# Bounds on the norms of float64 weights: TensorE products of bf16 halves in place of ScalarE squares, and low words of gate and value pieces made on ScalarE

## The chip, the cores and the metric

The kernel runs on one core of one Trainium2 chip. The metric is the device time of one execution in microseconds (us). "Faster", "same" and "slower" are meant against the kernel before, at 0.2% of its time.

## The reference, cut to what matters

Three blocks follow each other: an attention that drops scores below the row's maximum minus `tau`, a gated MLP behind an RMS norm, and a dense mixture of 8 experts weighted by a Sinkhorn-normalised table.

```python
# q, k, v: (4, 8, 576, 64) float32; tau = 0.02
scores = scale * q @ k.T                       # per batch and head
scores = where(scores >= rowmax - tau, scores, -1e9)
attn   = softmax(scores) @ v                   # x: 2304 tokens x 512
# w_gate, w_val: (512, 1536), w_out: (1536, 512), all float64; rms_g: 512
xn  = x / sqrt(mean(x*x) + 1e-6) * rms_g
x   = (silu(xn @ w_gate) * (xn @ w_val)) @ w_out
# 8 experts, w1: (8, 512, 1024), w2: (8, 1024, 512)
P   = exp(logits); 8 rounds of row and column normalisation
out = sum_e P[:, e:e+1] * (relu(x @ w1[e]) @ w2[e])
```

[...] The kernel builds float32 from the two 32-bit words of each element, scales by a power of two taken from a bound on the columns' norms, and splits each value into two float16 halves for TensorE.

## The kernel before, in words

The program has three stages, and the first two are merged by a scheduler that works at build time. It takes the instructions in a priority order, guesses when each is ready, and fixes the order of every engine's queue; on the chip each engine runs its queue strictly in that order. Only the third stage (the experts) has its TensorE order written out by hand.

**Attention.** 144 tiles (128 with one head and 128 queries, 16 with two heads and 64 remainder queries each). A tile is: scores `S` on TensorE (line 303), row maximum on VectorE (317), exponential on ScalarE (321), threshold on VectorE (323), a high half on ScalarE (328), a low half on GpSimd (329, 330), a transpose by DMA (340), and products with `v` on TensorE (360) four tiles later. When the 8 tiles of a token tile are done, `finish_x` normalises it (376 to 383) and transposes it into `xnT`.

**Preparation of the float64 weights.** `prep_in` runs six times (gate and value for each of three groups of 512 columns), each over four pieces of 128 x 512. For a piece, SyncE loads 512 KB into a `words` tile (four such tiles for gate and value), and `to_f32` makes float32: ScalarE takes the high words through Prelu (462), VectorE shifts the low words by 29 bits (463) and ors them in (465). ScalarE then squares the piece to bf16 (483), and TensorE multiplies with `gsq`, the squares of `rms_g`, into the PSUM bank `mx` (484), of which there is one. After four pieces VectorE takes the maximum of that bank (486) and makes a scale in five small steps (72 to 84), and the piece is written as two float16 halves (492 on ScalarE, 493 on VectorE). The float32 pieces stand in three stage buffers, which are thirds of the later `wo`. `prep_out` does the same for 12 pieces of `w_out`, with two single `words` buffers; its squares go through ScalarE's accumulator (517), and the pieces are rescaled and split at the end (534 VectorE, 535 ScalarE, 536 GpSimd).

**The gated MLP.** Nine tiles of 256 tokens. `mlp_in(j)` runs 12 column blocks `f` of 24 matmuls `gv` (557), followed by Tanh (565), two products (566, 567) and a split (571, 572); `mlp_out(j)` runs 2 x 36 matmuls (591). `mlp_in(0)` starts when the first two token tiles are in `xnT` and the first weight group is ready.

What sets the order around the change is therefore each engine's queue, and on TensorE that an instruction which waits holds everything behind it: scores, `v` products, norm products and `gv` stand in one queue.

## Time and profile before

| | |
|---|---|
| time, median of 3 runs | 2072.87 us (2071.28 to 2073.14) |
| the profiled execution's own time | 2072.64 us |
| its span, first to last instruction | 2070.8 us |
| mean granted TensorE clock | 0.976 of 2.4 GHz |
| busy: TensorE, VectorE, ScalarE, GpSimd | 94%, 78%, 63%, 65% of the span |

The shares are means over stages with different limits. The preparation lies in the first 175 us, attention and MLP together reach to about 602 us, the rest of the MLP to about 730 us, and the experts fill what is left. Matmuls are pipelined and their busy time is a union, so a TensorE that is busy is not one at its peak.

### The profile page before, as it was taken

The page shows a single profiled execution, that of the slowest core. Times are in us where ns is not written, and L with a number is a line of the kernel's source. Part 1 is how long each engine was busy: PE and PEld are TensorE (multiplying, and loading weights), DVE is VectorE, ACT ScalarE, POOL GpSimd, SP SyncE. Part 2 cuts the span into 40 slices and gives each one's busy share as a digit, 9 for nine tenths or more (in the row PEclk, how much of TensorE's full clock was granted, in tenths as well). Part 3 has the DMA queues.
Part 4 walks back from the last instruction along what each step waited for, and adds up shares of the span by engine and source line. Part 5 has one row for each costly group of instructions (what it writes and reads, how often), then busy time and mean ns, then how long its engine had stood idle before and what let it go on. Part 6 is the DMA issues. An engine that isn't in the chain of part 4 may idle for free.

```text
span 2070.8 us, 43792 instructions
## 1 busy us (share of the span) xinstructions
PE 1937.3 (94%) x16462; PEld 1445.0 (70%) x16462; DVE 1622.1 (78%) x3364; ACT 1297.6 (63%) x2804; POOL 1351.4 (65%) x1412
## 2 busy tenths in 40 slices
PE   1558899899999998999999999999999999999998
PEld 0246676777777766777777777777777777777777
DVE  6998777778754546998888888888887888888865
ACT  6998778878753365657555555555555555555542
POOL 0457664666654476777677777776777777777754
PEclk9569999999999999999999999999999999999999
DMA  9987878977748665334434433444443434334332
GB/s 296 261 177 128 163 160 147 184 129 139 129 83 213 144 158 169 110 118 143 128 120 134 131 116 119 130 131 127 128 139 122 122 117 143 120 120 128 105 97 82
DMA packets 373093, 290.46 MB, mean 140 GB/s; under 512 B 286160, under 2 KB 299344, under 8 KB 372880
## 3 DMA queue, kind: packets, MB, share of 16 engines
q1 hardware_dynamic: 371712, 285.81, 53.6%
q8 instruction: 129, 2.11, 0.4%
q0 software_dynamic: 640, 1.84, 0.3%
q14 instruction: 84, 0.69, 0.1%
q10 hardware_dynamic: 528, 0.02, 0.0%
HBM read 195.71 MB, written 21.23 MB: 105 GB/s over the span
## 4 chain that ended last, share of the span: by engine, by line
PE 65%; DVE 3%; POOL 1%; DMA 1%; issue 1%; ACT 1%; SPq 0%; DVEq 0%; POOLq 0%; ACTq 0%
PE P L1127 30%; PE X L1059 17%; PE Z L1059 13%; PE gv L557 3%; PE x L591 2%; DVE w L766 1%; DMA xo<-x2d 1%; DVE acc L1141 0%; SPq L871 0%; DVE h L1038 0%; PE logits L913 0%; DVE lg L1005 0%; POOL w2s L833 0%; DVE w1m L790 0%; POOL h L1038 0%
## 5 line engine op out<-in xcount | busy, mean ns | idle before, releaser
L1127 PE MATMUL P<-w,h 128*128 128x256 f16 x6048 | 769.9, 273 | 2.7 <-DVE acc L1141 1.8
L1127 PEld LDWEIGHTS <-h 128*128 128x128 f16 x6048 | 591.4, 98 | 145.7 <-issue 9.8
L1059 PEld LDWEIGHTS <-w 128*128 128x128 f16 x4032 | 394.6, 98 | 195.6 <-issue 4.6
L1137 DVE SCALAR_TENSOR_TENSOR acc<-P,coef,acc 128x256 f32<-128x256 f32 x882 | 409.7, 477 | 81.7 <-PE P L1127 73.0
L1059 PE MATMUL X<-xo,w 128*128 128x384 f16 x2304 | 437.7, 327 | 1.3 <-ACT u2b L1079 0.9
L1059 PE MATMUL Z<-xo,w 128*128 128x384 f16 x1728 | 327.7, 326 | 1.5 <-DMA xo<-x2d 1.5
L329 POOL TENSOR_TENSOR hl<-e,hl 128x512 f16<-128x512 f32 x144 | 172.9, 1201 | 193.7 <-ACT hl L328 135.6
L557 PE MATMUL gv<-xnT,wg 128*128 128x256 f16 x1296 | 162.9, 274 | 14.7 <-DVE u L567 13.4
L557 PE MATMUL gv<-xnT,wv 128*128 128x256 f16 x1296 | 165.0, 273 | 0.0
L557 PEld LDWEIGHTS <-wg 128*128 128x128 f16 x1296 | 124.7, 98 | 33.7 <-issue 16.0
L591 PE MATMUL x<-wo,tT 128*128 128x512 f16 x648 | 144.2, 379 | 0.0
L323 DVE SCALAR_TENSOR_TENSOR e<-S,nt,e 128x576 f32<-128x576 f32 x144 | 116.5, 811 | 28.5 <-ACT e L321 28.0
L557 PEld LDWEIGHTS <-wv 128*128 128x128 f16 x1296 | 125.5, 98 | 14.7
L317 DVE TENSOR_REDUCE nt<-S 128x1 f32<-128x576 f32 x144 | 106.7, 750 | 25.1 <-PE S L303 22.8
L360 PE MATMUL pv<-vs,eT 128*128 128x64 f16 (+1 forms) x2240 | 97.1, 200 | 30.9 <-DMA eT<-hl 30.8
L360 PEld LDWEIGHTS <-eT 128*128 128x128 f16 (+1 forms) x2240 | 87.3, 105 | 52.9 <-DMA eT<-hl 40.3
L572 POOL TENSOR_TENSOR tT<-u,tT 128x256 f16<-128x256 f32 x108 | 74.9, 695 | 69.7 <-ACT tT L571 69.6
L321 ACT ACTIVATE e<-S,nt,c 128x576 f32<-128x576 f32 x144 | 117.4, 818 | 0.0
L591 PEld LDWEIGHTS <-tT 128*128 128x128 f16 x648 | 62.1, 98 | 70.7
L328 ACT ACTIVATE hl<-e 128x576 f16<-128x576 f32 x144 | 96.8, 677 | 21.3 <-DMA eT<-hl 10.4
L303 PE MATMUL S<-kT,qT 128*128 128x288 f16 (+1 forms) x320 | 65.2, 310 | 26.3 <-DVE e L323 19.7
L766 DVE SCALAR_TENSOR_TENSOR w<-w1r,w_s,w 128x512 f16<-128x512 f32 x64 | 84.1, 1328 | 7.1 <-ACT w L765 7.0
(2536 smaller groups left out, 3623.2 us busy)
## 6 DMA issues: line engine op xcount, KB each, us to landing
xo<-x2s SPq DMA_DIRECT2D x319, 384.0 KB, 3.1
w1r<-in_moe_w_dram SPq DMA_DIRECT2D x17, 1024.0 KB, 5.0
w2r<-in_moe_w_dram SPq DMA_DIRECT2D x17, 1024.0 KB, 6.1
x2s<-xo SPq DMA_DIRECT2D x17, 384.0 KB, 2.8
wgatew<-in_moe_w_gate_dram SPq DMA_DIRECT2D x12, 512.0 KB, 5.6
wo<-in_moe_w_out_dram SPq DMA_DIRECT2D x12, 512.0 KB, 4.6
wvalw<-in_moe_w_val_dram SPq DMA_DIRECT2D x12, 512.0 KB, 5.1
qX<-qT SPq DMA_DIRECT2D x40, 128.0 KB, 2.7
```

Of the source, the lines that this page charges most:

```text
L317: V.tensor_reduce(mx, sv, AX.XY, ALU.max)
L321: A.activation(ev, sv, AF.Exp, bias=nt[:, 0:1], scale=st["c2"][:, c : c + 1])
L323: V.scalar_tensor_tensor(ev, sv, nt[:, 1:2], ev, ALU.is_ge, ALU.mult, accum_out=sums[:, slot : slot + 1])
L328: A.activation(hl[:, 0:S], e, AF.Copy)
L329: G.tensor_tensor(hl[:, S + REM :], e[:, 0 : NCH * P], hl[:, 0 : NCH * P], ALU.subtract)
L360: T.matmul(o, lhsT=a, rhs=r, start=n == 0, stop=n == len(mm) - 1)
L557: T.matmul(gv[:, a, :], lhsT=w[:, l, kk, f * P : (f + 1) * P], rhs=xt[:, r * KD + kk, :], start=n == 0, stop=n == 3 * KD - 1,)
L591: T.matmul(ps, lhsT=tT[f][:, l, o : o + P], rhs=wo[:, f, r, :], start=n == 0, stop=n == 3 * KF - 1,)
L766: V.scalar_tensor_tensor(dst[1], src, s, dst[0], ALU.mult, ALU.subtract)
L1059: T.matmul(ps, lhsT=w[:, a, l, kk, f * P : (f + 1) * P], rhs=xb[:, r * 2 + kk, :], start=n == 0 and j in (0, 1, 3), stop=n == 5, skip_grou ...
L1127: T.matmul(ps, lhsT=hs[u, ao, f][:, l, jj * P : (jj + 1) * P], rhs=w2[h][:, bo, r, f, :], start=n == 0 and j in (0, 1, 3), stop=n == 5, sk ...
L1137: main[True] = V.scalar_tensor_tensor(y, ps, coef[h][:, i : i + 1], y, ALU.mult, ALU.add)
```

## The change

The bound on the columns' norms is taken another way. `gram` multiplies each block of 128 columns with itself, on the high 16 bits of the float32 values, read as bf16 in steps of four bytes; 4 blocks of a piece, and all pieces of a group, add up in one 128 x 128 bank. No ScalarE square of the weights is left. `rms_g` is no longer inside the product: it is scaled by one power of two at the start (`gn`, `ig2`). Since the bank's row maximum now differs from partition to partition, `all_max` follows: one more TensorE product into the same bank `mx`, and one more VectorE reduction. For `w_out`, four pieces add up in a bank, so three reductions take the place of 12 accumulators. For gate and value, ScalarE makes the low words: a Copy of the upper 16 bits of each low word (one uint16 of every four) with a scale and a bias, written as int32. `w_out` keeps VectorE's shift. The scales of `k` and `q` share two buffers instead of having one for each batch.

```diff
+    gm = small([P, 1], "gmax")
+    V.tensor_reduce(gm, g_sb, AX.X, ALU.max, apply_absolute_value=True)
+    s_g, i_g0 = pow2_scale(all_max(gm, "gmx0", True), 1, 0, "rms")
+    gn = small([P, KD], "gn")
+    V.tensor_scalar(gn, g_sb, s_g[:, 0:1], None, ALU.mult)
...
+    def gram(ps, raw, first, last):
+
+        w = raw.bitcast(BF16).rearrange("p (n t) -> p n t", t=2)
+        for c in range(DM // P):
+            blk = w[:, c * P : (c + 1) * P, 1]
+            T.matmul(
+                ps, lhsT=blk, rhs=blk, start=first and c == 0, stop=last and c == DM // P - 1
+            )
+
+    def gram_bank(name):
+
+        return psx.tile([P, P], F32, tag="mx", name=name, bufs=1)
...
-        V.tensor_scalar(lw, word[:, :, 0], 29, None, ALU.logical_shift_right)
+        if engine is A:
+            half = word.bitcast(U16).rearrange("p n (w t) -> p (n w) t", t=4)
+            A.activation(lw, half[:, :, 1], AF.Copy, scale=2.0**-13, bias=2.0**-15 - 0.5)
+        else:
+            V.tensor_scalar(lw, word[:, :, 0], 29, None, ALU.logical_shift_right)
...
-            to_f32(raw[:, kk], wd, f"{name}l{gi}_{kk}")
-            sq = pw.tile([P, 2 * P], F32, tag="u", name=f"{name}q{gi}_{kk}", bufs=2).bitcast(BF16)
-            A.activation(sq, raw[:, kk], AF.Square)
-            T.matmul(ps, lhsT=gsq[:, kk : kk + 1].to_broadcast([P, P]), rhs=sq, start=kk == 0, stop=kk == KD - 1)
-        n2 = small([P, 1], name + "n2", bufs=2)
+            to_f32(raw[:, kk], wd, f"{name}l{gi}_{kk}", A)
+            gram(ps, raw[:, kk], kk == 0, kk == KD - 1)
+        n2 = small([P, 1], "wn2", bufs=2)
         V.tensor_reduce(n2, ps, AX.X, ALU.max)
-        s, inv = norm_scale(n2, 1, 9, f"{name}{gi}")
+        s, inv = norm_scale(all_max(n2, "wnx"), 1, 9, f"{name}{gi}")
...
-            sq = to_f32(wo32[:, f], wd, f"wol{f}").bitcast(BF16)[:, 0:DM]
-            A.activation(sq, wo32[:, f], AF.Square, accum_out=om[:, f : f + 1])
+            to_f32(wo32[:, f], wd, f"wol{f}")
+            if f % n == 0:
+                ps = gram_bank(f"wog{f}")
+            gram(ps, wo32[:, f], f % n == 0, f % n == n - 1)
+            if f % n == n - 1:
+                V.tensor_reduce(om[:, f // n : f // n + 1], ps, AX.X, ALU.max)
```

The scheduler orders all of attention and MLP anew. Three places show what matters; line numbers behind the change are the changed program's.

ScalarE's queue at the first gate pieces; before, `wgatew` is a loaded piece, `wo` the stage buffer, `wgateq` the squares, and `ks`, `qs`, `vmq` belong to attention's first batch:

```order
L462 ACTIVATE wo<-wgatew_0_884 128x512
L186 ACTIVATE vmq_0_210,vm<-raw_v_111 128x1024
L462 ACTIVATE wo<-wgatew_1_893 128x512
L483 ACTIVATE wgateq_0_890<-wo 128x512
L272 ACTIVATE qs_0_163<-raw_q_115,q_s 128x8x64
L241 ACTIVATE ks_0_0_172<-raw_k_107,k_s 128x4x64 x2
```

The same place in the changed program, where `wgatel` are the low words:

```order
L482 ACTIVATE wo<-wgatew_0_899 128x512
L485 ACTIVATE wgatel_0_901<-wgatew_0_899 128x512
L185 ACTIVATE vmq_0_225,vm<-raw_v_126 128x1024
L271 ACTIVATE qs_0_178<-raw_q_130,q_s 128x8x64
L240 ACTIVATE ks_0_0_187<-raw_k_122,k_s 128x4x64 x2
L482 ACTIVATE wo<-wgatew_1_909 128x512
```

Each square is replaced by a low-word copy of the same size, which reads the loaded piece and no longer waits for VectorE's or.

TensorE's queue of the changed program at the end of the first norm group; `wgaten` is the bank of the first gate group, `vmxp` the maximum of `v`, `wnxp` the new maximum over partitions, `wvaln` the bank of the value group:

```order
L455 LDWEIGHTS wo
L455 MATMUL wgaten_898<-wo 128x128
L133 LDWEIGHTS vmm
L133 MATMUL vmxp<-ident,vmm 128x128
L133 LDWEIGHTS wn_939
L133 MATMUL wnxp<-ident,wn_939 128x128
L455 LDWEIGHTS wo
L455 MATMUL wvaln_962<-wo 128x128
```

Between the two groups there stood nothing but `vmxp` before; now `wnxp` waits there for a VectorE reduction, and the first `wvaln` product for another, since all three use the bank `mx`.

ScalarE's queue around the first Tanh of the MLP (`u_0`), before; `wo<-wof` is the split of `w_out` (line 535):

```order
L535 ACTIVATE wo<-wof 128x512
L186 ACTIVATE vmq_1_2088,vm<-raw_v_1892 128x1024
L321 ACTIVATE e_2_7_1989<-S_2_7_1965,nt_2_7_1986,c_0_160 128x576
L535 ACTIVATE wo<-wof 128x512
L565 ACTIVATE u_0_1253<-gv_0_1228,g_0_995 128x256
L328 ACTIVATE hl_2_6_1959<-e_2_6_1955 128x576
L186 ACTIVATE vmq_2_2126,vm<-raw_v_1892 128x512
```

The same place in the changed program; `wo<-wo_1762` is a high-word conversion of a piece of `w_out`:

```order
L327 ACTIVATE hl_2_6_2064<-e_2_6_2060 128x576
L185 ACTIVATE vmq_1_2193,vm<-raw_v_1997 128x1024
L585 ACTIVATE u_0_1316<-gv_0_1291,g_0_1026 128x256
L327 ACTIVATE hl_2_7_2098<-e_2_7_2094 128x576
L185 ACTIVATE vmq_2_2231,vm<-raw_v_1997 128x512
L482 ACTIVATE wo<-wo_1762 128x512
```

The same attention tiles stand ahead of the first Tanh (tile 2_7 is the 24th), but three conversions and the whole split of `w_out` have moved behind it.

## Rows read from the trace of the kernel before

**Rows 1.** The page: span, and busy time of TensorE.

```profile
span 2070.8 us, 43792 instructions
PE 1937.3 (94%) x16462; PEld 1445.0 (70%) x16462; DVE 1622.1 (78%) x3364; ACT 1297.6 (63%) x2804; POOL 1351.4 (65%) x1412
```

**Rows 2.** Busy time by stretch: length, PE, PEld, DVE, ACT, POOL, PEclk, DMA share, GB/s.

```profile
50.00:110.00 60.00, 29.68 (x221) 16.42 (x222) 60.00 (x138) 55.33 (x114) 24.57 (x25) 0.54 0.97 249
110.00:143.50 33.50, 15.75 (x158) 10.25 (x158) 30.62 (x64) 29.27 (x67) 16.73 (x20) 0.55 0.98 202
143.50:196.00 52.50, 44.59 (x529) 37.80 (x526) 46.52 (x114) 48.88 (x120) 41.60 (x50) 1.00 0.63 112
196.00:400.00 204.00, 188.11 (x2055) 141.60 (x2053) 150.96 (x359) 160.92 (x371) 121.20 (x165) 1.00 0.85 163
400.00:602.00 202.00, 197.43 (x2259) 150.69 (x2258) 157.74 (x360) 155.59 (x362) 133.95 (x184) 0.99 0.76 135
760.00:2070.80 1310.80, 1296.69 (x10000) 973.84 (x9998) 1073.17 (x2087) 745.83 (x1563) 931.92 (x867) 1.00 0.40 124
```

**Rows 3.** Timeline of PE: start, length, what; first MLP matmuls, first output matmuls.

```profile
143.54 1.48 PE L557 MATMUL gv<-xnT,wg 128*128 128x256 f16 x12
...
196.08 3.83 PE L591 MATMUL x<-wo,tT 128*128 128x512 f16 x17
```

**Rows 4.** Groups of DVE by shape, 0 to 175 us: count, busy us, mean ns, idle before.

```profile
L465 DVE SCALAR_TENSOR_TENSOR wo<-wo,wol 128x512 int32<-128x512 int32 x12 | 10.5, 873 | 0.2
...
L463 DVE TENSOR_SCALAR wol<-wo 128x512 int32<-128x512 int32 x12 | 5.6, 471 | 1.6 <-DMA wo<-in_moe_w_out_dram 1.6
L463 DVE TENSOR_SCALAR wvall<-wvalw 128x512 int32<-128x512 int32 x12 | 5.2, 437 | 0.0
L463 DVE TENSOR_SCALAR wgatel<-wgatew 128x512 int32<-128x512 int32 x12 | 4.9, 420 | 3.6 <-DMA wgatew<-in_moe_w_gate_dram 3.6
...
L486 DVE TENSOR_REDUCE wgaten<-wgaten 128x1 f32<-128x512 f32 x3 | 2.0, 680 | 0.0
...
L136 DVE TENSOR_REDUCE kmx<-kmxp 128x1 f32<-128x128 f32 x2 | 0.6, 290 | 0.4 <-PE kmxp L134 0.4
```

**Rows 5.** Groups of ACT by shape, 0 to 700 us: the squares.

```profile
L517 ACT ACTIVATE wol<-wo 128x512 bf16<-128x512 f32 x12 | 7.5, 624 | 2.9 <-DVE wo L465 2.9
...
L483 ACT ACTIVATE wgateq<-wo 128x512 bf16<-128x512 f32 x12 | 7.2, 623 | 0.0
```

**Rows 6.** Timeline of ACT, two stretches of back-to-back work.

```profile
61.45 1.14 ACT L483 ACTIVATE wvalq<-wo 128x512 bf16<-128x512 f32 x2
...
63.11 1.21 ACT L462 ACTIVATE wo<-wgatew 128x512 f32<-128x512 f32 x2
...
105.63 0.64 ACT L517 ACTIVATE wol<-wo 128x512 bf16<-128x512 f32 x1
...
106.24 0.83 ACT L321 ACTIVATE e<-S,nt,c 128x576 f32<-128x576 f32 x1
106.96 0.67 ACT L462 ACTIVATE wo<-wo 128x512 f32<-128x512 f32 x1
```

**Rows 7.** Who PE waited for, 0 to 200 us: total us, times, longest.

```profile
PE wgaten L484 <- ACT wgateq L483: 12.9, 4, 9.0
...
PE wvaln L484 <- DVE wgaten L486: 4.8, 1, 4.8
PE S L303 <- DVE wval_i L72: 3.4, 1, 3.4
```

**Rows 8.** One line each of GpSimd and TensorE: ns min/median/max, first and last start.

```profile
L536 POOL TENSOR_TENSOR wo<-wof,wo x12: 1145/1153/1219, 143.0 to 174.1; 128x512 f16<-128x512 f32 x12
```

**Rows 9.** Line 134, the products of a maximum over partitions, same columns.

```profile
L134 PE MATMUL kmxp<-ident,kmm x4: 219/224/288, 14.1 to 355.7; 128*128 128x128 bf16 x4
```

**Rows 10.** Lines 462 and 451: conversions of `w_out`, and landing of the loads.

```profile
L462 ACT ACTIVATE wo<-wo x12: 644/667/673, 88.3 to 133.2; 128x512 f32<-128x512 f32 x12
...
DMA to landing us min/median/max: 3.7/5.2/9.1
```

More of the change, by code (lines that the diff above doesn't have):

```diff
@@ L11 @@
 I32 = mybir.dt.int32
+U16 = mybir.dt.uint16
 AF = mybir.ActivationFunctionType
@@ L62, in small, with pow2_scale @@
         return p0.tile(shape, dt, tag=name, name=name, bufs=bufs)
-    def pow2_scale(mx, n, bits, name, least=2.0**-100, root=False):
-        s = small([P, n], name + "_s")
-        inv = small([P, n], name + "_i")
+    def pow2_scale(mx, n, bits, name, least=2.0**-100, root=False, bufs=1):
+        s = small([P, n], name + "_s", bufs=bufs)
+        inv = small([P, n], name + "_i", bufs=bufs)
         if root:
@@ L105 @@
     G.dma_start(out=g_sb, in_=moe_rms_g.rearrange("(k p) -> p k", p=P))
-    gsq = small([P, KD], "gsq", BF16)
-    V.tensor_tensor(gsq, g_sb, g_sb, ALU.mult)
     tau8 = small([P, 1], "tau8")
@@ L166, in load_raw, with norm_scale @@
         return t
-    def norm_scale(sq, n, bits, name):
-        return pow2_scale(sq, n, bits, name, 2.0**-60, True)
+    def norm_scale(sq, n, bits, name, bufs=1):
+        return pow2_scale(sq, n, bits, name, 2.0**-60, True, bufs)
     def junk(name):
@@ L218, in prep_q_scales @@
         s_k, i_k = st["k"]
-        s_q, i_q = norm_scale(st["qm"], NW, 9, f"q{b}")
+        s_q, i_q = norm_scale(st["qm"], NW, 9, "q", 2)
         wt = small([P, NW], f"wt_{b}")
@@ L441 @@
     NG = DFF // DM
+    gm = small([P, 1], "gmax")
[3 more added lines that the diff above has]
+    V.tensor_scalar(gn, g_sb, s_g[:, 0:1], None, ALU.mult)
+    ig2 = small([P, 1], "ig2")
+    V.tensor_tensor(ig2, i_g0, i_g0, ALU.mult)
+    def gram(ps, raw, first, last):
[7 more added lines that the diff above has]
+        return psx.tile([P, P], F32, tag="mx", name=name, bufs=1)
     def words(src, name, tag="tT"):
@@ L452, in words, with to_f32 @@
         return r.rearrange("p (n w) -> p n w", w=2)
-    def to_f32(dst, word, name):
+    def to_f32(dst, word, name, engine=None):
         lw = pw.tile([P, 2, 2, HD], F16, tag="xs", name=name, bufs=2)
@@ L474, in prep_in @@
         staged[0] += 1
-        ps = psx.tile([P, DM], F32, tag="mx", name=f"{name}n{gi}", bufs=1)
+        ps = gram_bank(f"{name}n{gi}")
         cols = slice(gi * DM, (gi + 1) * DM)
@@ L480, in prep_in @@
             )
-            to_f32(raw[:, kk], wd, f"{name}l{gi}_{kk}")
-            sq = pw.tile([P, 2 * P], F32, tag="u", name=f"{name}q{gi}_{kk}", bufs=2).bitcast(BF16)
-            A.activation(sq, raw[:, kk], AF.Square)
-            T.matmul(ps, lhsT=gsq[:, kk : kk + 1].to_broadcast([P, P]), rhs=sq, start=kk == 0, stop=kk == KD - 1)
-        n2 = small([P, 1], name + "n2", bufs=2)
+            to_f32(raw[:, kk], wd, f"{name}l{gi}_{kk}", A)
+            gram(ps, raw[:, kk], kk == 0, kk == KD - 1)
+        n2 = small([P, 1], "wn2", bufs=2)
         V.tensor_reduce(n2, ps, AX.X, ALU.max)
-        s, inv = norm_scale(n2, 1, 9, f"{name}{gi}")
-        gs = small([P, KD], f"{name}gs{gi}")
-        V.tensor_scalar(gs, g_sb, s[:, 0:1], None, ALU.mult)
+        s, inv = norm_scale(all_max(n2, "wnx"), 1, 9, f"{name}{gi}")
+        gs = small([P, KD], "wgs", bufs=3)
+        V.tensor_scalar(gs, gn, s[:, 0:1], None, ALU.mult)
         for kk in range(KD):
@@ L502, in prep_group @@
         a = small([P, 1], f"g32_{gi}")
[L503 removed]
+        V.tensor_scalar(a, i_g, i_g0[:, 0:1], 1.0 / 32.0, ALU.mult, ALU.mult)
         g32.append(a)
[L505 removed]
+        V.scalar_tensor_tensor(igv[:, gi : gi + 1], i_g, ig2[:, 0:1], i_v, ALU.mult, ALU.mult)
     ixs = small([P, 1], "ixs")
@@ L512, in prep_out @@
         n = KF // NG
-        om = small([P, KF], "om")
+        om = small([P, NG], "om")
         for f in range(KF):
             wd = words(bits[f * P : (f + 1) * P, :], f"wo{f}", ("x2", "x2t")[f % 2])
-            sq = to_f32(wo32[:, f], wd, f"wol{f}").bitcast(BF16)[:, 0:DM]
-            A.activation(sq, wo32[:, f], AF.Square, accum_out=om[:, f : f + 1])
-        for _ in range(2):
-            V.tensor_tensor(
-                om.rearrange("p (g f) -> p g f", g=NG),
-                om.rearrange("p (g f) -> p g f", g=NG),
-                igv.to_broadcast([P, NG, n]),
-                ALU.mult,
-            )
+            to_f32(wo32[:, f], wd, f"wol{f}")
[4 more added lines that the diff above has]
+                V.tensor_reduce(om[:, f // n : f // n + 1], ps, AX.X, ALU.max)
+        for _ in range(2):
+            V.tensor_tensor(om, om, igv, ALU.mult)
         om1 = small([P, 1], "om1")
```

5 lines of the change are left out of this document (1 added, 4 removed).

## The prediction, made before the changed kernel ran

> **What bounds the kernel now.** I read the table by stretch first, then the timeline of TensorE at the stage borders, and then the waits. From 143.5 us on TensorE is the bound: it is busy 44.6 of 52.5, 188.1 of 204 and 197.4 of 202 us up to 602, and 1296.7 of 1310.8 us in the experts [rows 2]. What it does there is fixed, so an end that comes sooner needs a TensorE that is filled sooner. It is not filled before: in 50 to 143.5 it is busy 45.4 of 93.5 us, at a granted clock of 0.54 and 0.55, which mixes the levels of 1.2 and 2.4 GHz. There the others are the bound. VectorE is busy 60.00 of 60 us in 50 to 110 and 30.6 of the next 33.5; ScalarE 55.3 and 29.3 [rows 2]. The border between the two regimes is the first MLP product `gv` at 143.54 us [rows 3]. It waits for the second token tile of attention, which is made by ScalarE and VectorE in the same queues as the weights. I therefore price the change by what stands on these two queues ahead of that token tile, and follow the shift to the end.
>
> The order makes this simple. At the first `gv` TensorE has done the same attention in both programs (96 score matmuls, 280 `v` products). At the first output product of the MLP it again has the same (160 and 448), and at later ones it differs by at most two attention tiles. From within the seventh MLP tile on, TensorE's queue is the same row by row. So the change cannot alter what is left to do at the border, apart from 16 norm products; it alters when the border comes.
>
> **What stands ahead of the border, ScalarE.** I count instructions ahead of the second `xn` (line 382) in both orders.
> - The 12 squares of `w_out` with accumulator go. One takes 0.61 us of the queue, from 105.63 to the next start at 106.24 [rows 6]: -7.3 us.
> - 24 squares become 24 low-word copies. Two squares back to back take 1.14 us with 0.62 for one, so one costs 0.52 [rows 5, 6]. No row shows a copy from uint16 in steps of eight bytes to int32. Its nearest row is the Prelu, which reads the same loaded piece in the same steps: two take 1.21 us, one 0.67, so 0.55 [rows 6, 10]. Below, it cannot be cheaper than the square by anything the rows show; above, I take the step of the exponential, 0.72 us (106.24 to 106.96) for a larger tile. That gives 0 to +4.8 us; I take 0.55, the nearest: +0.7 us.
> - Five conversions of `w_out` pieces move behind the border: -2.8 us. One exponential moves ahead of it: +0.7 us.
>
> Sum: -7.3 + 0.7 - 2.8 + 0.7 = -8.7 us.
>
> **The same, VectorE.** The 24 shifts go, 4.9 + 5.2 = 10.1 us by busy time; five pieces of `w_out` move behind, each 0.47 + 0.87 us: 6.7. Six reductions fall from 0.68 to 0.29 us: 2.3. Seven new reductions over partitions and one of `w_out`, at 0.29, cost 2.3 [rows 4]. Sum: about -16.8 us; overlap of neighbours makes it less, but it stays well above ScalarE's. The nine small instructions on `rms_g` at the start fall before the first load, and hide behind the wait for `k`.
>
> So VectorE, now full, is relieved more than ScalarE, and ScalarE becomes the later one. ScalarE has 8.9 us idle in 50 to 143.5 [rows 2], 4.7 of it where VectorE is never idle. If all of that vanished, the border would come 17.6 us sooner; if none, 8.7; with the dear copy, 4.6. I take 10, near the middle value, since a filled ScalarE still waits for scores and loads.
>
> A rule of the Trainium skill speaks against this part. The rows say that a low word costs 0.42 to 0.44 us on VectorE and about 0.62 on ScalarE [rows 4, 5]. The page "ScalarE: Activation LUTs", section "Rules for kernel authors", says that cheap elementwise work belongs on VectorE and not on ScalarE; for one instruction the trace agrees. By the rule alone the shifts would stay: VectorE would then have -6.7 us and ScalarE some -22, and the border would come 6.7 us sooner instead of 8.7 to 10. What decides here is which queue is full, and so I do not follow it.
>
> **TensorE.** 24 products of 512 columns become 144 of 128 columns, with six times the weight loads, plus seven products over partitions. 128 of the 144 stand ahead of the border, where it has 48 us idle in 93.5. The 16 others stand among the first 144 `gv`. No row shows a stream of such pairs with both operands in steps of four bytes: a single product of 128 columns takes 0.219 us at the median [rows 9], so 3.5 us above; below, nothing, because the stretch has 7.9 us idle [rows 2]. I take 1 us. The Trainium skill, "TensorE: Matmul & The Clock Gate", section "Back-to-back issue gap", gives some 81 ns for 128 columns in a stream of loads and products; by it the 16 would take an estimated 1.3 us, and no run here shows it yet.
>
> **What moves behind the border.** The splits of `w_out` (lines 534 to 536) move behind the first Tanh, and five of the 12 GpSimd ones even behind the split of the twelfth MLP block, just ahead of the output product. They take 5 x 1.15 = 5.8 us there [rows 8]. The output product takes pieces in order: 17 matmuls start within 3.83 us [rows 3], so the seven pieces that are ready feed 21 matmuls or some 4.7 us, and it waits 0 to 2 us; I take 0.5. ScalarE and VectorE get their five conversions back in a stretch where neither is full (48.9 and 46.5 of 52.5 us), and TensorE has `gv` to do meanwhile.
>
> **Sum.** -10 + 1 + 0.5 = -8.5 us. The profiled execution took 2072.64 us, 1.8 more than its span [rows 1], and stands 0.2 under the median of 2072.87. So 2072.9 - 8.5 = 2064.4 us.
>
> **Rivals.** 0.2% is 4.1 us, and that is about what a measurement of this kernel tells from no change.
>
> *Given back, same.* The last norm product of `w_out` stands behind the 144th of 288 `gv`, and `gv` behind it waits. Conversions of `w_out` ran from 88.3 to 133.2, 4.1 us a piece, since two single buffers wait for loads that land after 5.2 us [rows 10]. Four pieces are left at the border, 16 us, while 144 `gv` take half of 52.5 us. For it: the three group banks and the maxima of batch 1's `k` and `v` wait for one bank. Against it: 10 us of slack. Should it lose 5 to 8 us, the time is 2069 to 2073.
>
> *More than forecast.* ScalarE's idle time goes as well, because the norm product no longer waits for a square: TensorE waited 12.9 us for `wgate` squares alone [rows 7]. The border comes 15 to 17.6 us sooner, the time is 2056 to 2060. Against it: most of that idle has other causes, and `gv` also waits for a DMA transpose.
>
> *The bank, slower.* Before, the bank was handed over six times, once a group, and two of these hand-overs held TensorE 4.8 and 3.4 us, with scores behind them [rows 7]. Now each group has two: maximum, product over partitions, maximum, next group. VectorE answers in the order of its queue, so each may take as long. Six more at the mean of 4.1 us are 24.6 us. TensorE has idle time to spend there, but scores stand behind, and attention with them. It decides when more than 12.6 us of the 24.6 reach the scores: then the time is above 2077, and 2089 if all do. For it: `wnxp` and the next group's first product stand behind each other on TensorE in four of the six groups. Against it: on VectorE only one to four instructions stand between a group's two maxima, and its queue is shorter by the shifts. A copy at twice the Prelu's price (24 x 0.55 = 13 us) would end at the same place; I count it here as a small part.
>
> **How the numbers follow.** Forecast, 2060 to 2068.7: 0.52. More than forecast: 0.12. Given back: 0.19. Slower, the bank or the copy: 0.17. So faster 0.64, same 0.19, slower 0.17. The range of 2056 to 2077 takes in all cases but the slow one and an edge of the large gain; the likeliest case has 2060 to 2068.7 for itself.
>
> **What would show it.** The low-word copy should take 0.62 to 0.67 us. The first `gv` should start near 133.5 us and the first output product near 187; from there to the end the distance should be that of before, some 1875 us. In 50 to 110 VectorE should have idle time and ScalarE almost none. The forecast is wrong if the first `gv` comes no sooner (then TensorE's waits name `wn` or VectorE's reductions), if it comes sooner but the output product does not (then the wait is for a norm product or a split of `w_out`), or if both come sooner and the shift is lost in 196 to 602 us, where 20.5 us of idle time may grow as well as shrink.

## The result: 0.67% slower, and the profile after

The changed kernel takes 2086.44 us (median of 4 runs, 2083.93 to 2091.90) against 2073.01 us beside it (4 runs, 2071.28 to 2075.68): a ratio of 1.0067, 95% interval 1.0044 to 1.0090. The forecast was 2064.4 us in a range of 2056 to 2077, so it was wrong in sign. A trace is one execution: that of the changed kernel took 2091.90 us, the highest of its four and 5.5 over the median; that of the kernel before, 2072.64, lies near its median. Where the two traces differ by 19.2 us, the medians differ by 13.4. The medians of the kernel before, taken anew beside the runs below, lie between 2073.0 and 2075.7 us, so each run's ratio is to the kernel before beside it.

The page of the changed kernel answers to [rows 1]. TensorE is busy 16.8 us longer with work that is the same but for the norm products, and the span is 19.2 us longer.

```profile
span 2090.0 us, 43948 instructions
PE 1954.1 (93%) x16589; PEld 1458.6 (70%) x16589; DVE 1617.4 (77%) x3357; ACT 1291.6 (62%) x2780; POOL 1348.2 (65%) x1412
```

Busy time by stretch, after, with the columns of [rows 2]:

```profile
50.00:110.00 60.00, 32.22 (x282) 21.02 (x282) 56.22 (x124) 52.77 (x106) 22.05 (x27) 0.65 1.10 251
110.00:143.50 33.50, 21.39 (x206) 14.88 (x204) 28.92 (x62) 28.26 (x60) 16.60 (x20) 0.61 1.05 212
143.50:196.00 52.50, 47.00 (x531) 38.97 (x530) 47.82 (x125) 44.50 (x109) 35.75 (x47) 0.93 0.63 127
196.00:400.00 204.00, 184.06 (x1974) 136.27 (x1973) 154.36 (x353) 158.74 (x366) 124.48 (x164) 0.96 0.83 156
400.00:602.00 202.00, 189.95 (x2085) 143.41 (x2084) 150.49 (x347) 150.25 (x349) 124.10 (x171) 0.99 0.70 131
```

Ahead of 143.5 us things are as forecast in kind: VectorE is no longer full (56.2 of 60). What is new stands below that: in 143.5 to 602 us the granted clock, 1.00, 1.00 and 0.99 in [rows 2], is 0.93, 0.96 and 0.99, and the rows count 4,590 matmuls there in place of 4,843. The first `gv` and the first output product, which answer to [rows 3], in the timeline of TensorE:

```profile
139.91 1.87 PE L577 MATMUL gv<-xnT,wg 128*128 128x256 f16 x8 [0.44 <-DMA xnT<-xn]
...
193.86 4.47 PE L611 MATMUL x<-wo,tT 128*128 128x512 f16 x19
```

They come 3.6 and 2.2 us sooner than before. From the start of the last of the 648 output products to the end it takes 1342.6 us before and 1344.7 after. So nearly all of the loss lies between the first `gv` and the last output product. That stretch in one row, first of the kernel before, then of the changed one:

```profile
143.50:728.20 584.70, 555.71 (x5771) 421.37 (x5768) 414.16 (x962) 410.35 (x942) 348.63 (x465) 1.00 0.75 146
```

```profile
139.90:745.30 605.40, 567.14 (x5782) 427.05 (x5783) 423.57 (x980) 411.36 (x941) 348.40 (x463) 0.97 0.71 143
```

It grew by 20.7 us: 9.3 us are idle time of TensorE (29.0 to 38.3), 11.4 are longer busy time, most of it at a lower clock. By an estimate, taking the share below full clock in stretches of 10 us times their length, the clock cost 1.7 us before and 15.1 after.

**One stall in detail.** The largest, in the timeline of TensorE after:

```profile
176.96 1.47 PE L577 MATMUL gv<-xnT,wg 128*128 128x256 f16 x12
...
183.11 0.38 PE L577 MATMUL gv<-xnT,wv 128*128 128x256 f16 x2
188.79 2.72 PE L577 MATMUL gv<-xnT,wg 128*128 128x256 f16 x12 [5.30 <-DVE u L587]
```

TensorE stands still for 5.30 us, and the next twelve `gv` take 2.72 us where twelve took 1.47 before it. Stretches of 2 us (length, PE busy, granted clock, DMA share, GB/s) show why: the clock goes from its level of 2.4 GHz to that of 1.2 during the pause and is back at 194 to 196 us.

```profile
182.00:184.00 2.00, 1.49 (x26) 1.00 0.00 0
184.00:186.00 2.00, 0.00 (x0) 1.00 0.37 75
186.00:188.00 2.00, 0.00 (x0) 0.83 0.61 122
188.00:190.00 2.00, 1.21 (x6) 0.50 0.67 150
190.00:192.00 2.00, 2.00 (x12) 0.50 0.32 63
192.00:194.00 2.00, 2.00 (x11) 0.50 0.18 38
194.00:196.00 2.00, 2.00 (x11) 0.97 0.95 204
```

`gv` waits there for VectorE to empty a PSUM buffer (`u`, line 587). VectorE was not idle; this stood ahead of that `u` in its queue:

```profile
180.63 1.06 DVE L222 TENSOR_SCALAR bt<-q_s,k_s,ntau 128x5 f32<-128x5 f32 x1
...
182.49 0.47 DVE L554 TENSOR_SCALAR wof<-wo,wosf 128x512 f32<-128x512 f32 x1
182.88 0.47 DVE L241 SCALAR_TENSOR_TENSOR ks<-raw_k,k_s,ks 128x256 f16<-128x256 f32 x1
...
183.73 0.47 DVE L554 TENSOR_SCALAR wof<-wo,wosf 128x512 f32<-128x512 f32 x1
184.13 1.37 DVE L241 SCALAR_TENSOR_TENSOR ks<-raw_k,k_s,ks 128x256 f16<-128x256 f32 x1
...
185.49 0.46 DVE L241 SCALAR_TENSOR_TENSOR ks<-raw_k,k_s,ks 128x256 f16<-128x256 f32 x1
...
187.73 0.68 DVE L405 TENSOR_TENSOR x<-pv,rsum 128x512 f32<-128x512 f32 x1
188.33 0.41 DVE L587 SCALAR_TENSOR_TENSOR u<-u,gv 128x256 f32<-128x256 f32 x1
```

`wof` is the split of `w_out`, `ks` and `bt` the preparation of attention's second batch. In the lines shown the split takes 0.94 us and the second batch 3.36, so the late `k` is the larger part of this stall. Before, the splits ran from 143.0 [rows 8] to 175 us, as the MLP began. Now GpSimd's part of them, answering to [rows 8], runs from 179.4 to 207.6:

```profile
L556 POOL TENSOR_TENSOR wo<-wof,wo x12: 1150/1156/1342, 179.4 to 207.6; 128x512 f16<-128x512 f32 x12
```

The second batch's `k` maximum is 26 us late too (its product over partitions starts at 172.2, not 146.3). Both meet the end of the first MLP tile.

### The profile page after: what moved, and what is told of

It is laid out like the page before. It is cut to its first block, busy times and chain, and to the rows that moved or that the text cites. A ratio compares the mean times of both kernels' runs of the same rounds, so it can differ in the third digit from the quotient of the medians.

```text
span 2090.0 us, 43948 instructions
## 1 busy us (share of the span) xinstructions
PE 1954.1 (93%) x16589; PEld 1458.6 (70%) x16589; DVE 1617.4 (77%) x3357; ACT 1291.6 (62%) x2780; POOL 1348.2 (65%) x1412
## 4 chain that ended last, share of the span: by engine, by line
PE 66%; DVE 4%; POOL 2%; issue 1%; ACT 1%; DMA 1%; SPq 0%; DVEq 0%; POOLq 0%; ACTq 0%
PE P L1147 29%; PE X L1079 16%; PE Z L1079 12%; PE gv L577 4%; PE x L611 3%; DVE w L786 1%; DMA xo<-x2d 1%; PE pv L359 1%; PE S L302 0%; DVE acc L1161 0%; SPq L891 0%; DVE h L1058 0%; POOL tT L592 0%; ACT h L1057 0%; DVE lg L1025 0%
## 5 line engine op out<-in xcount | busy, mean ns | idle before, releaser
L1147 PEld LDWEIGHTS <-h 128*128 128x128 f16 x6048 | 590.8, 98 | 147.9 <-issue 11.2
L328 POOL TENSOR_TENSOR hl<-e,hl 128x512 f16<-128x512 f32 x144 | 170.8, 1186 | 206.2 <-ACT hl L327 139.9
L327 ACT ACTIVATE hl<-e 128x576 f16<-128x576 f32 x144 | 97.2, 677 | 23.2 <-DVE e L322 13.4
```

Source lines behind the costliest of these rows:

```text
L327: A.activation(hl[:, 0:S], e, AF.Copy)
L328: G.tensor_tensor(hl[:, S + REM :], e[:, 0 : NCH * P], hl[:, 0 : NCH * P], ALU.subtract)
L1147: T.matmul(ps, lhsT=hs[u, ao, f][:, l, jj * P : (jj + 1) * P], rhs=w2[h][:, bo, r, f, :], start=n == 0 and j in (0, 1, 3), stop=n == 5, sk ...
```

## The experiments

Three theories. **A, lateness:** `w_out`'s norm products now stand in TensorE's queue and use the bank `mx`; so its scale, its splits and the second batch's `k` scale come late and meet `gv`. **B, interleave:** the scheduler deals attention and MLP anew whenever anything changes (in the change up to 24 score matmuls apart from before, until the 1885th `gv`), and each deal has its own stalls. **C, loads:** the DMA engines, busy 0.97 and 0.98 of the time in 50 to 143.5 us [rows 2], set the border. Orders below are counted in TensorE's queue, "late" by the product `womxp` that ends `w_out`'s norms (behind 88 score matmuls and 0 `gv` before, 128 and 192 in the change).

**e1: low words on ScalarE alone.**

```diff
-            to_f32(raw[:, kk], wd, f"{name}l{gi}_{kk}")
+            to_f32(raw[:, kk], wd, f"{name}l{gi}_{kk}", A)
```

> The kernel before with one part of the change: ScalarE makes the low words of gate and value pieces; the norms stay squares. In its queue the product womxp (end of w_out's norms) stands behind 92 score matmuls and ahead of gv, as before (88). Theory A (the norm products of w_out push its splits and batch 1's k scale behind the border, where they meet gv): womxp near 140 us, no stall of TensorE over 4 us between 143 and 400, time 2069 to 2077. Theory B (any new order of the queues scatters the time by 10 us or so): no relation to womxp, time anywhere from 2060 to 2095. Theory C (the DMA engines are full up to the border, so relief of VectorE and ScalarE brings it no sooner): first gv between 139 and 146 us. Rival to all: the low copies themselves are dear, then 2080 or more and ScalarE full in 50 to 110.

Measured: 2092.16 us, ratio 1.0079 (1.0061 to 1.0097). The first `gv` came at 150.36 us, 6.8 later than before: without the squares taken off, ScalarE is full (59.73 of 60 us in 50 to 110):

```profile
50.00:110.00 60.00, 27.16 (x200) 14.65 (x201) 52.22 (x110) 59.73 (x122) 18.44 (x22) 0.86 0.98 247
```

A was early here and the time was still bad, so A alone does not explain it. The rival of dear copies has its signs here (a time above 2080, ScalarE full): the copies, 0.66 us each, come on top of the squares and hold the border. B allowed any time from 2060 to 2095 in e1 to e4, so these four runs cannot speak against it. The traced execution of e1, at 2085.41 us, is the lowest of its six, 6.7 under the median.

**e2: norm products alone.**

```diff
-            to_f32(raw[:, kk], wd, f"{name}l{gi}_{kk}", A)
+            to_f32(raw[:, kk], wd, f"{name}l{gi}_{kk}")
```

> The change with VectorE's shift kept for all low words; norm products for all weights. womxp stands behind 120 score matmuls and 168 gv (the change: 128 and 192; before: 88 and 0). Theory A: womxp near 165 us, splits of w_out about 172 to 205, stalls with falls of the granted clock between 175 and 240, time 2080 to 2092. Theory B: anywhere from 2060 to 2095. Theory C: first gv between 139 and 146 us. If the low copies were the cause, the time would fall to 2073 or less.

Measured: 2087.83 us, 1.0061 (1.0049 to 1.0073), first `gv` at 142.02. As A expects: a stall of 4.0 us at 181.7 and five of 1.9 to 2.5 later. The copies are not what costs in the change: without them the time is the same within the intervals.

**e3: `w_out`'s squares kept on ScalarE.**

```diff
-            gram(ps, wo32[:, f], f % n == 0, f % n == n - 1)
+            A.activation(sq, wo32[:, f], AF.Square, accum_out=om[:, f : f + 1])
```

> The change, but w_out's norms are taken as before, by ScalarE's squares with accumulators; gate and value keep norm products and low copies. womxp stands behind 100 score matmuls and 48 gv. Theory A: womxp near 150 us, batch 1's k scale near 152, splits of w_out from about 155 to 185, fewer stalls, time 2066 to 2076, at least 8 us under the change. Theory B: anywhere from 2060 to 2095. Theory C: first gv between 139 and 146 us, since ScalarE has 7 us more again and it would not matter.

Measured: 2086.49 us, 1.0054 (1.0040 to 1.0067). A missed by 10 us: `womxp` came at 150.7 as expected, the splits ended at 189.1, and there were six stalls of 2.0 to 4.2 us from 188 us on all the same. The traced execution, at 2093.30 us, is the highest of its six, 6.8 over the median.

**e4: `w_out` issued ahead of the first MLP tile.**

```diff
-                tT = mlp_in(0)
                 prep_out()
+                tT = mlp_in(0)
```

> The change with one pair of calls in the other order: the preparation of w_out is issued ahead of the first MLP tile's gv, so it has the higher priority. Work is the same to the instruction. womxp stands behind 116 score matmuls and 120 gv (the change: 128 and 192), the splits begin at the 29th attention tile in place of the 34th. Theory A: womxp 10 us or so sooner than the change, time 2074 to 2084, between the two kernels. Theory B: anywhere from 2060 to 2095. Theory C: first gv between 139 and 146 us.

Measured: 2080.60 us, 1.0022 (1.0012 to 1.0032), inside A's range; first `gv` at 136.88. The same work as the change, 5.8 us less by the order of two calls.

**e5 and e6: late, but with before's interleave from the 552nd `gv` on.** Ahead of it their order differs from before's by up to 8 score matmuls at a `gv` and 12 at an output product. Both were picked for their order alone.

```diff
-            to_f32(raw[:, kk], wd, f"{name}l{gi}_{kk}", A)
+            to_f32(raw[:, kk], wd, f"{name}l{gi}_{kk}", A if name == "wval" else None)  # e5, with e4's edit
+            to_f32(raw[:, kk], wd, f"{name}l{gi}_{kk}", A if gi > 0 else None)          # e6
```

> The change with two edits: ScalarE makes the low words of value pieces only (VectorE shifts those of gate), and the preparation of w_out is issued ahead of the first MLP tile. Chosen by its order alone: from the 552nd gv on TensorE's queue is row for row that of the kernel before (in the change it is not, before the 1885th), while the product womxp still stands late, behind 128 score matmuls and 182 gv. Theory B (what costs is how attention and MLP are interleaved behind the border, which each edit deals anew): from first to last output product 529 to 538 us as before (532.2; the change 551.4), time 2062 to 2074. Theory A (the late splits of w_out and the late k scale of batch 1 cost): stalls and a fallen clock between 175 and 240 us as in the change, 545 us or more, time 2080 to 2090. Both: first gv 137 to 143 us.

> The change with one edit: in the first of the three column groups VectorE shifts the low words, ScalarE makes them in the other two. TensorE's queue rejoins that of the kernel before at the 552nd gv; womxp stands behind 124 score matmuls and 192 gv, as late as in the change. Theory B: from first to last output product 529 to 538 us, time 2062 to 2074. Theory A: 545 us or more, time 2080 to 2090. Both: first gv 134 to 143 us (92 score matmuls stand ahead of it, not 96).

Measured: 2083.42 us, 1.0047 (1.0032 to 1.0062), and 2081.25 us, 1.0041 (1.0028 to 1.0054). The times are A's and not B's: with before's interleave behind the 552nd `gv` the loss stays. From first to last output product they take 542.0 and 543.5 us, between B's 538 and A's 545. Most of the loss lies from the first `gv` to the 145th output product (207.9 and 206.4 us, before 195.0). That place does not tell A from B, since e7, where nothing is late, takes 206.4 us for it too.

**e7: the kernel before, with another interleave and nothing else.** e4's edit, made to the kernel before.

> The kernel before with the preparation of w_out issued ahead of the first MLP tile: no instruction is added, removed or changed, and the preparation stands where it stood (womxp behind 88 score matmuls, all 12 splits at the same attention tiles); from the first output product on attention and MLP are interleaved otherwise (it stands behind 168 score matmuls, not 160). Theory B: from first to last output product 538 to 552 us, time 2078 to 2092. Theory A: 530 to 536 us, time 2069 to 2077, as before.

Measured: 2082.14 us, 1.0036 (1.0023 to 1.0049). Not an instruction is added or changed, the preparation stands where it stood, and 8.6 us are lost. The stretch from first `gv` to last output product, and after it TensorE's longest wait in 140 to 640 us (total, times, longest):

```profile
144.40:739.40 595.00, 559.67 (x5769) 422.95 (x5767) 418.78 (x962) 411.31 (x942) 346.78 (x465) 0.99 0.72 144
```

```profile
PE gv L557 <- DVE u L567: 20.4, 11, 4.4
```

That wait is 12.7 us, longest 2.6, in the kernel before. The time is in B's range and not in A's. From first to last output product it missed B's (535.9 us, not 538 to 552) and lies in A's, since 6.5 us of the loss came between `gv` and the first output product. B is real: an order alone cost 0.36%. The TensorE queue of e7 is that of the change, row for row, from the 767th `gv` on.

**e8 and e12: half of the float64 loads.** The edit is the same in the change and in the kernel before.

```diff
+            if kk % 2 == 0:
                 wd = words(...)
```

> The change without every second load of a float64 piece; the piece ahead of it is converted in its place, so all conversions and products stay and 9.4 MB of 18.9 are not loaded, and the output is another. Theory C (the DMA engines, busy 0.97 to 1.05 of the time to 143 us, set the border): first gv at 128 us or sooner. Against C: first gv 135 to 141 us. Its queue on TensorE rejoins that of the kernel before at the 552nd gv, so theory B: from first to last output product 529 to 538 us.

> The kernel before without every second load of a float64 piece (the piece ahead of it is converted in its place, so the output is another). If the DMA engines set the border before the change: first gv at 130 us or sooner. If not: 137 to 144 us. womxp stands early (84 score matmuls), and attention and MLP are interleaved otherwise than before: from first gv to last output product 590 to 598 us by theory A with B.

Measured in one run each: first `gv` at 140.20 (the change 139.91) and 143.43 (before 143.54). In e12 the DMA share in 50 to 110 us fell to 0.71 and VectorE stayed at 60.00 of 60:

```profile
50.00:110.00 60.00, 26.27 (x215) 15.35 (x215) 60.00 (x128) 53.75 (x114) 24.28 (x25) 0.56 0.71 159
```

So C is refuted in both: a DMA share of 0.97 was no bound. In the kernel before, VectorE was the full engine, and stayed it; no run shows by itself that its queue sets the border. e8 is also early (`womxp` behind 88 score matmuls) with before's interleave, and took 2070.96 us: the operations of the change, where neither A nor B holds, end no later than before, though with half the loads and in a single run (the kernel before beside it 2070.43 to 2078.39).

**e9: no norm work at all.**

```diff
-        V.tensor_reduce(n2, ps, AX.X, ALU.max)
-        s, inv = norm_scale(all_max(n2, "wnx"), 1, 9, f"{name}{gi}")
+        V.memset(n2, 1.0)
+        s, inv = norm_scale(n2, 1, 9, f"{name}{gi}")
```

> The change with all norm work of the float64 weights left out: no norm products, no products over partitions for gate and value, no maxima of them; the scales come from constants, so the output's scaling is not that of the reference. Low words stay on ScalarE. If norm products and their bank hold TensorE's queue (34 us of its waits to 140 us name them in the change), the first gv starts at 132 us or sooner. If the border is a chain through attention (transposes, exponentials, thresholds) that norm work does not stand on, first gv 136 to 141 us, where all forms of the change have it.

Measured in one run: first `gv` at 132.29 us, 0.3 beyond the first range, so norm work does hold the border: 7.6 us of it against the change. But the output product starts at 197.03, later than before (196.08 [rows 3]), and the run took 2079.53 us. A border 11.3 us sooner was worth nothing 65 us later, one stall of 5.5 us (at 151.5, scores behind VectorE's threshold) among the reasons.

**e10 and e11: early, with another interleave.** e10 keeps the norm products, with fewer low words on ScalarE; e11 is e3 with the first group's low words shifted by VectorE; both with e4's edit.

```diff
+            to_f32(raw[:, kk], wd, f"{name}l{gi}_{kk}", A if gi > 0 and name == "wval" else None)  # e10
+            to_f32(wo32[:, f], wd, f"wol{f}", A if f > 7 else None)                                # e10
+            to_f32(raw[:, kk], wd, f"{name}l{gi}_{kk}", A if gi > 0 else None)                     # e11
```

> The change with all its norm products, fewer low words on ScalarE (value pieces of groups 1 and 2, and the last four of w_out), and w_out's preparation issued first. Chosen by its order: womxp stands behind 104 score matmuls and 48 gv (the change 128 and 192), batch 1's k scale at 104 and 72; attention and MLP are interleaved otherwise than before until the 1885th gv. Theory A (late w_out splits and k scale cost most of it): from first gv to last output product 588 to 598 us (before 584.7, the change 605.4, the two early ones with another interleave 591.2 and 594.9), first gv 137 to 143 us, time 2067 to 2077. Theory B alone (the interleave only): 598 to 608 us, time 2079 to 2090.

> The change with w_out's squares kept on ScalarE, the first group's low words shifted by VectorE, and w_out's preparation issued first. womxp stands behind 96 score matmuls and 33 gv, nearly as before (88 and 0). Theory A: from first gv to last output product 588 to 598 us, first gv 137 to 143 us, time 2067 to 2077. Theory B alone: 598 to 608 us, time 2079 to 2090.

Measured: 2085.24 us, 1.0043 (1.0028 to 1.0058), and 2085.04 us, 1.0050 (1.0032 to 1.0067). The two signs point apart. The times miss A's range by 8 us and lie in that of B alone, while the stretch from first `gv` to last output product (597.0 and 597.2 us) lies within A's, at the upper end, and 1 us under B's. These two runs do not decide. In e10 the border came at 145.4 us, 2.4 beyond the range.

**e13 and e14: the kernel before, made late.** One buffer for `w_out`'s loaded pieces instead of two; e14 adds e4's edit. The kernel before, e7, e13 and e14 have the same instructions.

```diff
-            wd = words(bits[f * P : (f + 1) * P, :], f"wo{f}", ("x2", "x2t")[f % 2])
+            wd = words(bits[f * P : (f + 1) * P, :], f"wo{f}", ("x2", "x2t")[0])
```

> The kernel before with one buffer for w_out's loaded pieces in place of two: no instruction is added or removed. Its order puts womxp behind 124 score matmuls and 192 gv, as late as in the change, while TensorE's queue is row for row that of the kernel before from the 552nd gv on. Theory A (late splits of w_out and late k scale of batch 1 cost time wherever they come from): splits end 60 to 75 us after the first gv, from first gv to last output product 597 to 606 us (before 584.7), time 2080 to 2092. Theory B alone (only the interleave): 583 to 590 us, time as before, 2069 to 2077. If only the operations of the change cost (dear copies, norm products): as before too.

> The kernel before with one buffer for w_out's pieces, and w_out's preparation issued ahead of the first MLP tile: late (womxp behind 124 and 168) and with another interleave of attention and MLP until the 1885th gv (at gv and output products up to 40 score matmuls apart from before). The same instructions as before. Theories A and B together: the worst of the four, 600 to 612 us from first gv to last output product, time 2084 to 2096. B alone: as the kernel before with another order only, 590 to 598 us, 2079 to 2086.

Measured: 2079.07 us, 1.0024 (1.0014 to 1.0034), and 2091.69 us, 1.0085 (1.0071 to 1.0099). The stretch of e13, then of e14:

```profile
135.60:734.40 598.80, 559.74 (x5783) 423.27 (x5784) 428.65 (x987) 418.64 (x963) 348.46 (x465) 0.99 0.74 147
```

```profile
135.60:748.30 612.70, 567.44 (x5784) 428.24 (x5785) 418.86 (x987) 420.20 (x963) 352.33 (x465) 0.98 0.73 144
```

| first `gv` to last output product, us | interleave of before from the 552nd `gv` on | another |
|---|---|---|
| `w_out` early | 584.7 (before) | 595.0 (e7) |
| `w_out` late | 598.8 (e13) | 612.7 (e14, not e7's: up to 36 score matmuls apart) |

In this stretch lateness costs 14.1 us (e13, whose order ahead of the 552nd `gv` also differs from before's, by up to 12 score matmuls) and another interleave 10.3 (e7). In e14 both are changed, to an interleave that is not e7's, so its 28.0 us cannot be shared out. B alone is refuted by e13 (598.8 where it allowed 583 to 590), A alone by the time of e7. In the whole time lateness costs less: e13 is 0.24% slower, e7 0.36%. The time of e13 is a little under its range, because its border comes at 135.61 us, 7.9 sooner than before, though no instruction was saved: `w_out`'s conversions left the queues ahead of the border (and 92 score matmuls stand there, not 96). More than that is lost behind it. In the change, too, conversions of `w_out` moved behind the border, so part of its 3.6 us may be work put off and not saved; that part was not measured.

**e15: the change's norm products, early, with before's interleave.**

```diff
+            to_f32(raw[:, kk], wd, f"{name}l{gi}_{kk}", A if gi > 0 else None)
-        i_g = prep_in(moe_w_gate, wg, gi, "wgate")
         i_v = prep_in(moe_w_val, wv, gi, "wval")
+        i_g = prep_in(moe_w_gate, wg, gi, "wgate")
-                tT = mlp_in(0)
                 prep_out()
+                tT = mlp_in(0)
```

> All norm products of the change; VectorE shifts the low words of the first group, ScalarE makes them in the other two; value pieces are prepared ahead of gate pieces; w_out's preparation is issued first. Chosen by its order: womxp behind 100 score matmuls and 70 gv (the change 128 and 192), and TensorE's queue that of the kernel before from the 552nd gv on (in between at most 8 score matmuls apart). Theories A and B together: from first gv to last output product 585 to 594 us, first gv 137 to 142 us, time 2064 to 2074, faster than the change by 12 us or more, and not slower than the kernel before. If the operations of the change cost by themselves: 597 us or more, 2079 to 2090.

Measured: 2078.14 us, 1.0016 (1.0004 to 1.0027). Faster than the change by 8.3 us, where 12 were expected, and 3.3 slower than before, which is under 0.2% but clear of noise; the time misses its range by 4. The stretch is in range:

```profile
140.90:734.40 593.50, 563.69 (x5795) 426.81 (x5796) 421.93 (x980) 413.08 (x944) 348.51 (x466) 0.98 0.71 146
```

It is less early than its order looked: `womxp` came at 153.3 us (before 138.3), the splits ended 53 us behind the first `gv` (before 32). No kernel of the study with all of the work beats the kernel before.

**All runs in one view.** By when the last split ends in the traces, in us behind the first `gv`: within 35 (before, e1, e7, e8, e12) the stretch takes 584.7 to 595.0 us; at 45 to 53 (e3, e10, e11, e15) 593.5 to 607.0; at 59 and more (the change, e2, e4, e5, e6, e9, e13, e14) 598.3 to 612.7. Less idle time, and less the time lost to the clock, each of the 17 profiles leaves 550 to 556 us: close to the same work, and the rest is stalls and what the clock made of them. The groups overlap, and a trace stands up to 6.8 us from its median (e1 under, e3 over), so they show a trend and no border of a few us. e3 at 607.0 is the one for which lateness is no sufficient reason; what its six stalls share is open.

**Where the loss lies.** At the 577th `gv`, the first of the third MLP tile, the kernels of this table have done the same: 256 score matmuls, 840 `v` products and 144 output products.

| us | first `gv` to the 577th | from there to the last output product | TensorE's queue behind |
|---|---|---|---|
| before | 147.2 | 437.5 | before's |
| e13 | 162.2 | 436.6 | before's |
| e15 | 153.7 | 439.9 | before's |
| e6 | 158.7 | 441.1 | before's |
| e5 | 160.3 | 442.9 | before's |
| e7 | 153.3 | 441.7 | the change's, from the 767th `gv` on |
| the change | 157.0 | 448.4 | the change's |

The two parts in rows, of the kernel before, the change, e7 and e13:

```profile
143.50:290.80 147.30, 132.90 (x1452) 100.63 (x1449) 112.94 (x272) 119.32 (x279) 95.42 (x123) 1.00 0.77 148
290.80:728.20 437.40, 422.81 (x4321) 320.74 (x4320) 301.22 (x690) 291.03 (x665) 253.21 (x342) 1.00 0.75 145
139.90:296.90 157.00, 140.24 (x1462) 104.69 (x1463) 124.55 (x296) 123.02 (x282) 97.90 (x124) 0.94 0.75 151
296.90:745.30 448.40, 426.90 (x4322) 322.36 (x4321) 299.02 (x684) 288.33 (x659) 250.50 (x340) 0.99 0.70 141
144.40:297.70 153.30, 135.88 (x1449) 102.11 (x1447) 118.03 (x278) 122.03 (x283) 97.56 (x126) 0.98 0.77 146
297.70:739.40 441.70, 423.79 (x4321) 320.85 (x4320) 300.75 (x684) 289.27 (x659) 249.22 (x340) 1.00 0.70 143
135.60:297.90 162.30, 138.19 (x1464) 103.37 (x1465) 126.76 (x297) 127.77 (x300) 95.54 (x123) 0.96 0.76 150
297.90:734.40 436.50, 421.55 (x4321) 319.90 (x4320) 301.89 (x690) 290.87 (x664) 252.91 (x342) 1.00 0.73 146
```

All of e13's loss lies in the first two tiles, 15.0 us, and 7.9 of it is only the earlier start: it reaches the 577th `gv` 7.1 us after the kernel before. e7 loses 6.1 us there. Behind it, traces with before's queue spread from 436.6 to 442.9 us, so e7's 4.2 us more than before do not stand out. The change loses 9.8 us in the first part and 10.9 in the second, where it takes 6.7 more than e7 with nearly the same queue; its trace is 5.5 us over its median. How its loss is shared between lateness, interleave and this one execution is therefore not shown. What is shown is that an order costs 0.24 to 0.85% with not an instruction changed (e7, e13, e14).

## Why the prediction was wrong

**What bounds the kernel: right, with a gap.** e12 confirms that VectorE is full and that the loads are not the bound. But I read the border as the length of two queues. The sign that I gave for it failed: in 50 to 110 us VectorE does have idle time, 3.8 us, but ScalarE, which was to have almost none, has 7.2 (before 4.7). Relieved of its work, VectorE's queue gave way to another chain: followed back from the first `gv` as the page does from the last instruction, VectorE's share falls from 53.6 to 25.1 us, DMA rises from 34.0 to 46.9 (28.1 of it transposes, and 8.4 loads of weights that did not stand on it before), ScalarE from 23.8 to 30.7.

**The sizes of the operations: right.** The low copy, forecast at 0.62 to 0.67 us, and the small reductions, in groups by shape:

```profile
L485 ACT ACTIVATE wgatel<-wgatew 128x512 int32<-128x512 uint16 x12 | 7.8, 650 | 0.0
L489 DVE SCALAR_TENSOR_TENSOR wo<-wo,wgatel 128x512 int32<-128x512 int32 x12 | 8.5, 719 | 3.5 <-ACT wgatel L485 3.5
L507 DVE TENSOR_REDUCE wn<-wgaten 128x1 f32<-128x128 f32 x3 | 0.9, 284 | 0.6 <-PE wgaten L455 0.6
L135 DVE TENSOR_REDUCE wnx<-wnxp 128x1 f32<-128x128 f32 x6 | 1.7, 280 | 0.0
```

The rule of the Trainium skill ("ScalarE: Activation LUTs", "Rules for kernel authors") to use VectorE and not ScalarE for operations such as `max`, `add` and `mul`, carried over to the shifts, is not what decides: keeping the shifts there (e2) gave 2087.83 us, the change 2086.44. The border came 1.5 us sooner than before in e2, where the prediction had 6.7 by that rule, and 3.6 in the change.

**The border, -10 us: mis-sized, measured -3.6.** The second `xn` came 6.2 us sooner (130.9 after 137.1), not 8.7 to 10. TensorE's waits in 0 to 140 us, first a second line of the kernel before beside [rows 7], then the changed kernel's, show that its norm products wait as much as before, only for VectorE's `or` (15.9 + 11.2 us) in place of ScalarE's square (12.9 + 11.7):

```profile
PE wvaln L484 <- ACT wvalq L483: 11.7, 4, 5.3
```

```profile
PE wgaten L455 <- DVE wo L489: 15.9, 5, 10.3
PE pv L359 <- DMA eT<-hl: 12.4, 11, 3.0
PE wvaln L455 <- DVE wo L489: 11.2, 6, 4.6
...
PE wnxp L133 <- DVE wn L507: 4.3, 4, 2.5
```

**TensorE +1 and the moved splits +0.5: right in sum by luck, wrong in kind.** From first `gv` to first output product it took 54.0 us, 1.5 more than before (52.5). The 16 norm products behind the border take some 0.9 us, an estimate from the 55 ns below, but the output product did wait for no split. What I did not cost is that the splits, and the second batch's `k` behind them, now stand ahead of `u` in VectorE's queue: "where neither is full" was a mean over 52.5 us, and the 5.30 us were lost within it.

**"From there to the end the distance should be that of before": the step that failed.** The first output product came 2.2 us sooner and the end 19.2 later; the distance was 1896.1 us, not some 1875. I took the same matmuls behind the border for the same time. In truth their time hangs on the order of the queues: with the instructions of the kernel before, the stretch from the first `gv` to the last output product took 10.3 us more in e7 and 14.1 in e13; in the change it took 20.7 more. I had compared the interleave at the tiles' borders only, where it is at most two attention tiles apart; in between it is up to six (24 score matmuls), and up to four (16) in the first two tiles, where e7 and e13 lose most. The text named this loss as one that could show ("the shift is lost in 196 to 602 us"), but gave it no price, and "may grow as well as shrink" treated as even what was not: of the 15 kernels with whole loads that were profiled, the kernel before has the least idle time in this stretch and loses the least to the clock, and every new order found more. Which feature of the order costs most in the change stays open.

**The rivals.** "The bank" was on the right side by luck, by another way: `wnxp` and its bank cost TensorE 4.3 and some 4 us of waits ahead of the border, not 24.6. Most of what made `w_out` late are its norm products: without them (e3) `womxp` comes at 150.7 us, with them at 170.8, before the change at 138.3. Whether by the one bank or by their place in TensorE's queue was not told apart. They are not all of it: in e9, without any norm work, GpSimd's splits still begin at 156.8 us, before at 143.0. "Given back" foresaw `gv` waiting for `w_out`'s last norm product; the only waits of TensorE in 143 to 210 us are 5.5 us for `u`.

## What to carry to other kernels

When a scheduler deals the queues anew, a saving ahead of a border is worth only what the order behind it leaves: make a change that alters the order and nothing else first (e7: 0.36%), and take its loss as a measure of what "the same work" can cost, not as a bound (e14, the same instructions in a third order: 0.85%). A trace is one execution: say how far it lies from the median before reading a few us out of it. Ask of every piece of work that moves not only whether its reader waits, but what stands behind it in each queue that it enters; a mean of idle time over the stretch does not answer that. And where TensorE is the bound, price a stall with what may follow it: the 5.30 us stall of the change was followed by some 6 us at half clock.

## What the runs showed of the hardware that was not expected

A DMA share of 0.97 in a stretch was no sign of a bound: with half the loads it fell to 0.71, and the border moved by 0.1 us. Stalls cost the clock, but their sum does not say how much: by the estimate above the changed kernel has 38.3 us of idle time in 605 and lost 15.1 us to the clock, the kernel before 29.0 in 585 and 1.7, and e13 39.1 in 599 and 6.7. Nor does the length of one: in the kernel before, a pause of TensorE of 2.58 us from 155.1 on left the granted clock at 1.00 (157.6 to 161.6 us); in the change it was 0.57 behind one of 2.39 us from 361.9 on (364.3 to 368.3). The norm products, weight load and product both with operands in steps of four bytes, are cheap: four stand within 0.22 us at a granted clock of 1.00 (start to start of the first of them and of the score matmul behind them, 163.53 and 163.75):

```profile
163.53 0.39 PE L455 MATMUL wog<-wo 128*128 128x128 bf16 x4
163.75 0.41 PE L302 MATMUL S<-kT,qT 128*128 128x288 f16 x2
```

That is 55 ns for 128 columns. The Trainium skill, "TensorE: Matmul & The Clock Gate", section "Back-to-back issue gap", has some 81 ns for such a pair in a stream; in this short run the measurement is lower, and it decides.
